# Moving one unit's cluster masks ahead of its products in four of a pair's six periods

## The chip, the cores and the metric

The kernel runs on one core of one Trainium2 chip. The metric is the device time of one execution in microseconds (us). Before the change the median of 3 runs is 947.51 us, from 947.37 to 947.69.

Five engines work beside each other on a core. PE is the matrix engine; the profile lists its weight loads apart, as PEld. DVE, ACT and POOL work on vectors, and SP issues most of the transfers. Each engine takes its instructions in the order in which they were written, and semaphores tie the engines together. PE multiplies a stationary operand (the weights, `lhsT`) with a moving one (`rhs`); the result goes to PSUM, where it can be added to what stands there (`start=False`). A matmul that contracts over 64 or 32 partitions takes 64 or 32 of the array's 128 rows only, so that two or four such matmuls in different rows can run at once. The profile writes the form of the weights as rows\*columns: 64\*128, 32\*128, 128\*32.

## The reference

Two blocks follow each other. The first is a clustered attention over 4 batches of 8 heads, with 768 positions of 64 values; the second is a gated feed-forward layer over the 3072 tokens, 512 to 2048 to 512, all in float32.

```python
q_assign = np.argmax(np.einsum('bhsd,hcd->bhsc', q_n, c_n), axis=-1)   # 16 clusters
k_assign = np.argmax(np.einsum('bhsd,hcd->bhsc', k_n, c_n), axis=-1)
mask = q_assign[:, :, :, None] == k_assign[:, :, None, :]
scores = scale * np.matmul(q, k.transpose(0, 1, 3, 2))
scores = np.where(mask, scores, -1000000000.0)
scores = scores - np.max(scores, axis=-1, keepdims=True)
attn = np.exp(scores)
attn = attn / (np.sum(attn, axis=-1, keepdims=True) + 1e-09)
out = np.matmul(attn, v)
...
h = x @ w_in
sp = np.maximum(h, 0.0) + np.log1p(np.exp(-np.abs(h)))
return (h * erf(sp)) @ w_out
```

## The kernel before

The attention works on 16 pairs of heads, numbered p from 0 to 15; the two heads of a pair lie in partitions 0 to 63 and 64 to 127 (`e` is 0 or 1). A pair has 12 units: a unit is one block of 128 keys (`j`) against one half of the queries (384 columns). A period handles two units, `u` and `u + 1`, so a pair has six periods, `i` from 0 to 5.

Per unit and head there are four steps on PE.

- `products` (line 546): the products of queries and keys, float32, 64 rows for each head, 384 columns. It opens the sum in the PSUM tile `sc` (`start=True`). A float32 matmul shows as two in the profile.
- `scores` (line 559): the cluster masks. `km` and `qm` hold, in bfloat16, one row for the shift (the negated maximum of the query's row) and rows that take a huge number off where the clusters differ. It adds to `sc` and closes it. With `rows=Q` it takes 32 rows for each head: rows 0 to 31 and 64 to 95. In the first period of all and in the last four it takes 64 (`rows=D`).
- `curve` (line 573): the exponential on ACT, from `sc` into `pr`.
- `attend` (line 594): the products with the values, weights of 128 rows and 32 columns, one period later. For every half, `divide` adds the products that give the sums and divides.

The shift needs the row maxima of the masked scores before the exact products exist. They are found ahead, by `maxima_step` (line 459), from a bfloat16 copy of queries and keys. A step has a pass of products (`qv` with `kv`, 64 rows for each head), then a mask pass (`qm` with `km`) onto the same PSUM tile `wide`, then a reduction on DVE that reads `wide`. Of `wide` there is one, so each step's first pass waits for the reduction of the step before. A period makes two steps. As first step of a period stands, in most periods, the remaining 256 keys of one block of queries, as second step the first 512 (or 384) of the next one. The steps run about seven ahead, so those of the later periods belong to the next pair, whose `qv`, `kv`, `qm` and `km` are other tiles.

`maxima_step` is a generator. With `behind=False` its mask pass takes 64 rows for each head. With `behind=True` it stops after the first pass, and its mask pass then takes rows 32 to 63 and 96 to 127 alone, where the masks lie a second time; so `scores` in rows 0 to 31 and 64 to 95 can run beside it.

The order of the work is written out by hand in `period` (line 1393); nothing plans it anew. On PE a period of the pairs 1 to 15 runs like this: the first step (both passes, 64 rows), `products(u)`, `products(u + 1)`, the second step's first pass, `scores(u)` beside the second step's mask pass, `scores(u + 1)`, and then `attend` of the two units before. Small masks of the next pair stand between (`masks`, line 429; table `MASKS`, line 55): in period 2 one between the two products in 64 rows, and one after `scores(u + 1)` in 32 rows (`turned<-hotT,pick`). The tile `sc` has two buffers, one for each unit of a period. Every call passes through a helper at line 127, so the profile shows that line for nearly everything; the names of the tiles tell the steps apart.

After the attention the feed-forward layer runs on PE with weights of 128 rows; the change does not touch it.

Of the kernel before, what the change touches and what calls it, by code (L numbers as in the profile page):

```python
# [9 lines left out]
F32 = mybir.dt.float32  # L10
# [9 lines left out]
P = 128  # L20
B, H, S, D = 4, 8, 768, 64
C = 16
NJ = S // P
Q = 32
NB = S // Q
HW = S // 2
QW = HW // 2
TW = QW + 1
HJ = NJ // 2
# [106 lines left out]
def kernel(  # L136
# [37 lines left out]
    def passing(name, bufs, **kw):  # L174
        return attention.enter_context(tc.tile_pool(name=name, bufs=bufs, **kw))

    ps_s = passing("ps_s", 2, space=PSUM)
# [30 lines left out]
    rows = [{nm: const.tile([P, S], F32, name=f"{nm}T{i}") for nm in "qk"} for i in range(2)]  # L208
# [124 lines left out]
    for e in range(2):  # L333
        for n in range(2):
            r = e * D + n * Q
# [37 lines left out]
    def transposes(p, which="qk"):  # L373

        if p >= NPAIR:
            return
        st = pairs[p]
        for nm in which:
            st[nm + "T"] = rows[p % 3][nm]
            ve.transpose(out=st[nm + "T"], in_=st.pop(nm).rearrange("p n t -> p (n t)"))  # L380
        if "k" in which:
            st.update(lows[p % 2])
            if p > 1:
                load_qk(p + 1)
# [44 lines left out]
    def masks(p, nm, half, bank, narrow=False, copied_by=ae):  # L429

        if p >= NPAIR:
            return lambda: None
        st = pairs[p]
        cols = slice(half * HW, (half + 1) * HW)
        r, hot = slice(0, D) if nm == "q" else slice(D, P), st["hotT"]
        picked = pick[r, half]
        if narrow:
            r = slice(r.start + Q, r.stop)
            picked = pick[r, 1]
            hot = hot if half else st["aside"]  # L440
        won = bank[:, 0:HW]
        te.matmul(won, lhsT=picked, rhs=hot[r], start=True, stop=True)
        if nm == "q":
            return lambda: ae.activation(out=st["qm"][:, cols], in_=won, func=ACT.Relu)
        if copied_by is ve:
            return lambda: ve.tensor_scalar(
                out=st["km"][:, cols], in0=won, scalar1=BIG, scalar2=nbig, op0=ALU.mult, op1=ALU.add
            )
        return lambda: ae.activation(
            out=st["km"][:, cols], in_=won, func=ACT.Identity, bias=nbig, scale=BIG  # L450
        )
# [3 lines left out]
    def pieces_of(i, keys_of):  # L455
        t, part = divmod(i, 2)
        return ((t, part, *((0, keys_of[t]), (keys_of[t], S))[part]),)
# [84 lines left out]
    units = [(p, half, j) for p in range(NPAIR) for half in range(2) for j in range(NJ)]  # L542

    sc_of = {}

    def products(u):
        p, half, j = units[u]
        if u in sc_of:
            return
        st = pairs[p]  # L550
        sc = sc_of[u] = ps_s.tile([P, 2, 512], F32, name="sc", tag="s")
        for e in range(2):
            r = slice(e * D, (e + 1) * D)
            te.matmul(
                sc[:, e, 0:HW], lhsT=st["kT"][r, j * P : (j + 1) * P],
                rhs=st["qT"][r, half * HW : (half + 1) * HW], start=True, stop=False,
            )

    def scores(u, rows=Q):

        p, half, j = units[u]
        st = pairs[p]
        sc = sc_of[u]
        assert ("shift", half) in st
        for e in range(2):
            r = slice(e * D, (e + 1) * D)
            r = slice(r.start, r.start + rows)
            te.matmul(
                sc[:, e, 0:HW], lhsT=st["km"][r, j * P : (j + 1) * P],
                rhs=st["qm"][r, half * HW : (half + 1) * HW], start=False, stop=True,  # L570
            )

    def curve(u):
# [795 lines left out]
    def run(work):  # L1369
        for _ in work:  # L1370
            pass
# [3 lines left out]
    def step_ahead(p, i, behind=False):  # L1375
        if p == 0 and i < NJ:
            steps = maxima_step(0, pieces_of(NJ + i, FIRST_KEYS), behind=behind, by_products=True)
        elif p == 0 and i < NJ + len(JOINED):
            steps = maxima_step(1, JOINED[i - NJ], behind=behind)
        else:  # L1380
            p, i = divmod(2 * NJ * p + NJ + 1 + i, 2 * NJ)
            steps = maxima_step(p, pieces_of(i, KEYS), behind=behind) if p < NPAIR else iter(())
        if not behind:
            run(steps)
        return steps
# [7 lines left out]
    def period(p, i):  # L1393
        u = 2 * NJ * p + 2 * i
        n1, n2 = 2 * p - 1, 2 * p
        early = lambda n: 0 <= n < N_EARLY

        def mask(place):
            which = (MASKS if p else FIRST_MASKS).get((i, place))
            if which:  # L1400
                return masks(p + 1, *which, turned[0 if i in (0, 5) else 1], place == 2)
            return lambda: None

        if u > 0:
            for which in turns if i in (0, 3) else ():
                turn(*which)
                turns.remove(which)
            if i == 3 and not p:
                transposes(2, "k")
            if i == 3 and p:  # L1410
                similarities(p + 2)
                routing[0] = choose(p + 2, turned[0], True)
            step_ahead(p, 2 * i)
            if i == 3 and p:
                next(routing[0], None)
            if i == 2:
                transposes(p + 2, "k" if p else "q")
        mask(0)()
        if i == 0 and early(n1 - 1):
            sign(n1 - 1)  # L1420
        elif i == 3 and early(n1):
            sign(n1)
        if i == 4:
            next(routing[0], None)
        next(part[0], None)
        if i == 0 and p:
            run(routing[0])
            transposes(p + 2, "q")
        if u == 2:
            next(routing[0])  # L1430
        products(u)
        mask(3)()
        products(u + 1)
        mask(1)()
        second = step_ahead(p, 2 * i + 1, True) if u > 0 else iter(())
        next(second, None)
        rows = D if u == 0 or u + NJ + 2 >= len(units) else Q
        scores(u, rows)
        next(second, None)
        next(second, None)  # L1440
        next(part[0], None)
        if i == 5 or u == 2:
            next(routing[0], None)
        scores(u + 1, rows)
        later = mask(2)
        if i == 3 and not p:
            similarities(p + 2)
            routing[0] = choose(p + 2, turned[0], True)
        if i == 0:
            later()  # L1450
            curve(u)
        else:
            curve(u)
            later()
        curve(u + 1)
        if u == 0:
            step_ahead(0, 1)
            similarities(1)
            routing[0] = choose(1, turned[1])
            next(routing[0])  # L1460
            vectors(1, "q")
            vectors(1, "k")
        if i == 0 and early(n1 - 1):
            bounded(n1 - 1)
            shifted(n1 - 1)
        elif i == 1 and early(n1):
            size_and_rest(n1)
        elif i == 5 and early(n2):
            rest(n2)
        for _ in range(FORMS.get(p, {}).get(i, 0)):  # L1470
            x_forms.pop(0)() if x_forms else forms.pop(0)[0]()
        if i == 3:
            if not p:
                next(routing[0], None)
            if early(n1):
                bounded(n1)
                shifted(n1)
        elif i == 1:
            load(p + 1, "v", v, vp)
            if p == 0:  # L1480
                run(routing[0])
        elif i == 4:
            vectors(p + 2, "k")
            vectors(p + 2, "q")
        if u > 0:
            if i == 1 and early(n1 - 1):
                summed(n1 - 1)
            elif i == 4 and early(n1):
                summed(n1)
            if i in POOL_FORMS.get(p, ()) and forms:  # L1490
                forms.pop(0)[1]()
            for w in (u - 2, u - 1):
                accumulate(w)
            for w in (u - 2, u - 1):
                attend(w)
            if i == 3:
                next(routing[0], None)
            if i % HJ == 0 and u - 1 != LATE or u - 3 == LATE:
                part[0] = divide(u - 1 - u % NJ)
                next(part[0])  # L1500
        if i == 3 and early(n2):
            size(n2)
# [11 lines left out]
    st = pairs[0]  # L1514
# [56 lines left out]
    u = len(units)  # L1571
# [13 lines left out]
    behind = pool("behind", 1).tile([P, 1], F32, name="behind")  # L1585
# [87 lines left out]
```

## Time and profile before

| what | value |
|---|---|
| median of the runs | 947.51 us |
| the profiled execution's own time | 948.0 us |
| its span, from first to last instruction | 946.3 us |
| granted PE clock | 1.00 |
| PE busy | 939.0 us (99% of the span) |
| DVE busy | 785.0 us (83%) |
| ACT busy | 547.2 us (58%) |
| POOL busy | 505.6 us (53%) |
| attention, first unit's products to the last period's | 8.9 to 396.0 us |
| six periods of one pair (p = 7 to p = 8) | 23.9 us |

A row of the timeline gives the start and the length in us, the engine, the operation, output and inputs by name, the weights' rows\*columns, the moving operand and how many such instructions were joined. The ends of matmuls are modelled and overlap with the next ones; so the text works with the differences of starts. Products with keys and queries that lie in the third set of buffers show as `sc<-more_out`.

### The profile page before, as it was taken

What the parts mean: (1) busy time and instruction counts of PE and PEld (TensorE: products, weight loads), DVE (VectorE), ACT (ScalarE), POOL (GpSimd) and SP (SyncE); (2) the same over time, 40 slices, a digit from 0 to 9 for tenths busy, and PEclk for the clock granted to TensorE, in tenths of its full rate; (3) what the DMA queues carried; (4) which work ended last, traced back from release to release, by engine and by line L of the source; (5) the groups of instructions that cost most, each with busy time, mean ns of one, the idle gap of its engine ahead of it and who ended that gap; (6) DMA issues with size and microseconds to landing.
All of it is one profiled execution on the core that took longest, in us unless ns stands there. A gap on an engine that the chain in (4) does not pass through costs nothing.

```text
span 946.3 us, 22340 instructions
## 1 busy us (share of the span) xinstructions
PE 939.0 (99%) x8764; PEld 708.1 (75%) x8764; DVE 785.0 (83%) x1420; ACT 547.2 (58%) x809; POOL 505.6 (53%) x357
## 2 busy tenths in 40 slices
PE   8999999999999999999999999999999999999998
PEld 3555555555555555588888888998999899989987
DVE  7888888888888887869886688689868977897887
ACT  3677777777777777476423543653257236525541
POOL 1688888888888888999118211450063016103600
PEclk9999999999999999999999999999999999999999
DMA  9354455445443621133876248353454336343533
GB/s 217 73 114 112 112 113 111 112 112 111 113 113 69 157 58 36 26 120 124 216 224 238 100 122 214 109 179 112 156 167 135 133 119 206 113 154 123 157 112 111
DMA packets 176352, 123.17 MB, mean 130 GB/s; under 512 B 132600, under 2 KB 143352, under 8 KB 176248
## 3 DMA queue, kind: packets, MB, share of 16 engines
q1 hardware_dynamic: 171880, 116.34, 43.1%
q0 software_dynamic: 1872, 4.98, 3.0%
q8 instruction: 69, 1.13, 0.5%
q10 hardware_dynamic: 2496, 0.43, 0.2%
q14 instruction: 35, 0.29, 0.1%
HBM read 91.78 MB, written 23.33 MB: 122 GB/s over the span
## 4 chain that ended last, share of the span: by engine, by line
PE 98%; DVE 1%; ACT 0%; issue 0%; DVEq 0%
PE bank L127 43%; PE turned L127 32%; PE sc L127 17%; PE wide L127 6%; DVE nmx L127 1%; ACT qm L127 0%; DVE sims L127 0%; ACT km L127 0%; DVE hotT L127 0%; DVE wide L127 0%; DVE hot L127 0%; DVE nbig L127 0%; DVE osb L127 0%; DVEq L1668 0%; DVE lowest L127 0%
## 5 line engine op out<-in xcount | busy, mean ns | idle before, releaser
L127 POOL TENSOR_TENSOR more_out<-more_out,pr 128x768 f32<-128x768 f32 x128 | 217.2, 1697 | 15.8 <-ACT pr L127 6.1
L127 DVE TENSOR_REDUCE nmx<-wide 128x2 f32<-128x512 f32 (+2 forms) x189 | 179.1, 948 | 46.9 <-PE wide L127 45.9
L127 ACT ACTIVATE pr<-sc 128x768 f32<-128x768 f32 x192 | 148.5, 810 | 80.5 <-PE wide L127 73.0
L127 PE MATMUL turned<-pr,in_v 128*32 128x193 f32 x3072 | 145.2, 330 | 0.0
L127 POOL TENSOR_TENSOR g<-g 128x512 f32<-128x512 f32 x36 | 47.2, 1310 | 180.7 <-DVE g L127 178.8
L127 PEld LDWEIGHTS turned<-pr,in_v 128*32 128x32 f32 x3072 | 90.2, 109 | 51.3 <-issue 27.3
L127 DVE TENSOR_TENSOR g<-g 128x512 f32<-128x512 f32 x132 | 90.8, 688 | 22.9 <-PE bank L127 12.2
L127 PE MATMUL sc<-qT,kT 64*128 64x384 f32 x528 | 98.5, 485 | 0.0
L127 DVE TENSOR_TENSOR g<-bank,g 128x256 f32<-128x256 f32 (+1 forms) x128 | 64.7, 531 | 18.1 <-PE bank L127 9.4
L127 PE MATMUL bank<-g_more,g 128*128 128x256 f32 (+1 forms) x328 | 75.8, 374 | 0.0
L127 PE MATMUL bank<-x_own,w_in 128*128 128x128 f32 (+1 forms) x440 | 74.0, 309 | 0.0
L127 ACT ACTIVATE a_s<-g 128x1024 f32<-128x1024 f32 x38 | 39.7, 1056 | 58.0 <-POOL g L127 45.3
L127 POOL TENSOR_TENSOR more_out<-pr,pr 128x768 f32<-128x768 f32 x32 | 59.6, 1864 | 20.1 <-ACT pr L127 20.1
L127 PEld LDWEIGHTS bank<-g_more,g 128*128 128x128 f32 x328 | 61.1, 190 | 8.4 <-DVE g L127 0.4
L127 DVE TENSOR_TENSOR g<-a_s,g 128x512 f32<-128x512 f32 x76 | 65.9, 888 | 0.9 <-ACT a_s L127 0.9
L127 PEld LDWEIGHTS bank<-x_own,w_in 128*128 128x128 f32 x440 | 63.2, 191 | 4.4 <-issue 0.6
L127 PE MATMUL wide<-kv,qv 64*128 64x256 bf16 (+2 forms) x378 | 64.8, 327 | 0.9 <-ACT km L127 0.6
L127 PE MATMUL bank<-w_out,g 128*128 128x256 f32 x280 | 64.5, 379 | 0.0
L127 PEld LDWEIGHTS <-qv 64*128 64x128 bf16 x384 | 23.1, 93 | 52.8 <-issue 37.8
L127 PE MATMUL wide<-km,qm 64*128 64x256 bf16 (+4 forms) x378 | 62.3, 326 | 0.0
L127 ACT ACT_TABLE_LOAD x40 | 51.3, 1283 | 17.6 <-DVE g L127 17.0
L127 PEld LDWEIGHTS sc<-qT,kT 64*128 64x128 f32 x528 | 46.3, 187 | 19.1 <-issue 1.8
(244 smaller groups left out, 1993.0 us busy)
## 6 DMA issues: line engine op xcount, KB each, us to landing
g_more<-b_dram SPq DMA_DIRECT2D x52, 512.0 KB
g_more<-w_dram SPq DMA_DIRECT2D x84, 256.0 KB
x_own<-in_moe_w_in_dram SPq DMA_DIRECT2D x13, 512.0 KB
in_v<-in_v_dram SPq DMA_DIRECT2D x32, 192.0 KB
x_dram<-more_out SPq DMA_DIRECT2D x128, 48.0 KB
x_own<-x_dram SPq DMA_DIRECT2D x6, 1024.0 KB
in_k<-in_k_dram SPq DMA_DIRECT2D x59, 96.0 KB
in_q<-in_q_dram SPq DMA_DIRECT2D x58, 96.0 KB
```

What stands on the lines that cost most here:

```text
L127: ins = getattr(self.engine, name)(*args, **kw)
```

## The change

`scores` may now open the sum in `sc` (`ahead=True`: `start=True`, `stop=False`), and `products` may close it (`behind=True`). In `period` a flag `ahead` is true for p > 0 in the periods 1, 2, 4 and 5, as long as the units left are more than eight. There the first maxima step is made with `behind=True` as well: after its first pass come the masks of unit `u` (`scores(u, Q, True)`) in rows 0 to 31 and 64 to 95, and beside them the step's mask pass in rows 32 to 63 and 96 to 127 instead of in 64 rows. `products(u, True)` then adds to `sc` and closes it. In the block after the products, the second step's mask pass now has `scores(u + 1)` beside it, and no second pair of masks follows. The numbers of instructions stay as they are on every engine; only PE's order changes. The periods 0 and 3, pair 0 and the last four periods are as before.

```diff
+    def score_banks(u):
+        if u not in sc_of:
+            sc_of[u] = ps_s.tile([P, 2, 512], F32, name="sc", tag="s")
+        return sc_of[u]
+
-    def products(u):
+    def products(u, behind=False):
         p, half, j = units[u]
-        if u in sc_of:
+        if u in sc_of and not behind:
             return
         st = pairs[p]
-        sc = sc_of[u] = ps_s.tile([P, 2, 512], F32, name="sc", tag="s")
+        sc = score_banks(u)
...
-                rhs=st["qT"][r, half * HW : (half + 1) * HW], start=True, stop=False,
+                rhs=st["qT"][r, half * HW : (half + 1) * HW], start=not behind, stop=behind,
...
-    def scores(u, rows=Q):
+    def scores(u, rows=Q, ahead=False):
...
-                rhs=st["qm"][r, half * HW : (half + 1) * HW], start=False, stop=True,
+                rhs=st["qm"][r, half * HW : (half + 1) * HW], start=ahead, stop=not ahead,
...
+        more = u + NJ + 2 < len(units)
+        ahead = p > 0 and i % HJ > 0 and more
...
-            step_ahead(p, 2 * i)
+            step = step_ahead(p, 2 * i, ahead)
+            next(step, None)
+            if ahead:
+                scores(u, Q, True)
+            run(step)
...
-        products(u)
+        products(u, ahead)
         mask(3)()
         products(u + 1)
         mask(1)()
         second = step_ahead(p, 2 * i + 1, True) if u > 0 else iter(())
         next(second, None)
-        rows = D if u == 0 or u + NJ + 2 >= len(units) else Q
-        scores(u, rows)
+        rows = Q if u > 0 and more else D
+        scores(u + ahead, rows)
         next(second, None)
         next(second, None)
...
-        scores(u + 1, rows)
+        if not ahead:
+            scores(u + 1, rows)
```

More of the change, by code (lines that the diff above doesn't have):

```diff
@@ L555, in products @@
                 sc[:, e, 0:HW], lhsT=st["kT"][r, j * P : (j + 1) * P],
-                rhs=st["qT"][r, half * HW : (half + 1) * HW], start=True, stop=False,
+                rhs=st["qT"][r, half * HW : (half + 1) * HW], start=not behind, stop=behind,
             )
-    def scores(u, rows=Q):
+    def scores(u, rows=Q, ahead=False):
         p, half, j = units[u]
         st = pairs[p]
-        sc = sc_of[u]
+        sc = score_banks(u)
         assert ("shift", half) in st
```

## The prediction

> **What bounds the kernel now.** I read the page first: who is busy, at what clock, and what the chain that ended last consists of.
>
> ```profile
> span 946.3 us, 22340 instructions
> PE 939.0 (99%) x8764; PEld 708.1 (75%) x8764; DVE 785.0 (83%) x1420; ACT 547.2 (58%) x809; POOL 505.6 (53%) x357
> PE 98%; DVE 1%; ACT 0%; issue 0%; DVEq 0%
> ```
>
> PE carries 98% of that chain. Then the busy time by stretches inside the attention, and the waits between 45 and 385 us:
>
> ```profile
> 200.00:250.00 50.00, 50.00 (x703) 26.38 (x703) 43.11 (x73) 38.24 (x58) 43.79 (x28) 1.00 0.51 112
> ...
> PEld L127 <- issue: 66.4, 180, 0.6
> DVE nmx L127 <- PE wide L127: 42.7, 63, 1.5
> PEld turned L127 <- issue: 24.4, 72, 0.4
> ```
>
> The first row gives the stretch, its length, and the busy time of PE, PEld, DVE, ACT and POOL, then the granted clock. PE is busy for 50.00 of 50 us at a clock of 1.00, while DVE (43.11), ACT (38.24) and POOL (43.79) have room. DVE waits for PE (`nmx <- wide`), and matmuls wait for no engine for long; only weight loads stand still, by "issue", for 66.4 and 24.4 us. So in this stage a period is as long as PE's sequence. A busy PE isn't PE at its peak, so the starts inside one period have to say what that sequence is made of. This is PE in period 5 of pair 7, up to the next period's first pass; then its weight loads:
>
> ```profile
> 207.53 0.28 PE L127 MATMUL wide<-kv,qv 64*128 64x256 bf16 x2
> 207.65 0.27 PE L127 MATMUL wide<-km,qm 64*128 64x256 bf16 x2
> 207.75 1.46 PE L127 MATMUL sc<-qT,kT 64*128 64x384 f32 x8
> 209.05 0.38 PE L127 MATMUL wide<-kv,qv 64*128 64x512 bf16 x2
> 209.36 0.34 PE L127 MATMUL sc<-qm,km 32*128 32x384 bf16 x2
> 209.37 0.39 PE L127 MATMUL wide<-km,qm 32*128 32x512 bf16 x2
> 209.53 0.33 PE L127 MATMUL sc<-qm,km 32*128 32x384 bf16 x2
> 209.79 1.51 PE L127 MATMUL turned<-pr,in_v 128*32 128x193 f32 x32
> 211.23 0.28 PE L127 MATMUL wide<-kv,qv 64*128 64x256 bf16 x2
> ```
>
> ```profile
> 207.52 0.10 PEld L127 LDWEIGHTS <-qv 64*128 64x128 bf16 x2 [0.31 <-issue]
> ...
> 207.65 0.95 PEld L127 LDWEIGHTS sc<-qT,kT 64*128 64x128 f32 x8
> 208.73 0.26 PEld L127 LDWEIGHTS <-qv 64*128 64x128 bf16 x2
> 209.35 0.09 PEld L127 LDWEIGHTS <-km 32*128 32x128 bf16 x2 [0.36 <-issue]
> 209.78 0.32 PEld L127 LDWEIGHTS turned<-pr,in_v 128*32 128x32 f32 x12 [0.32 <-issue]
> ```
>
> Two things are to be seen. First, what a stream costs when the form of the weights stays: 256 columns take 0.10 to 0.12 us (207.53 to 207.65 to 207.75), 384 columns 0.17 (209.36 to 209.53), so 512 about 0.21 (by proportion). Second, what it costs when the form changes. The 512-column pass from 209.05 should end at 209.26, and the next matmul, in form 32\*128, starts at 209.36: 0.10 more. The 384 columns from 209.53 should end at 209.70, and `attend` in form 128\*32 starts at 209.79: 0.09. Every weight load of a new form has an "issue" wait before it (0.31, 0.36, 0.32 us) and starts with its matmul; loads of the same form, such as `qT,kT` at 207.65, were made under the matmul before. So a **change of form** empties the array, and three kinds of it (128\*32 to 64\*128, 64\*128 to 32\*128, 32\*128 to 128\*32) cost some 0.09 to 0.10 us each.
>
> The same numbers stand in the first and the last of the 57 periods that change (14 pairs by four, and period 1 of pair 15):
>
> ```profile
> 47.92 0.28 PE L127 MATMUL wide<-kv,qv 64*128 64x256 bf16 x2
> 48.15 1.46 PE L127 MATMUL sc<-qT,kT 64*128 64x384 f32 x8
> 49.44 0.38 PE L127 MATMUL wide<-kv,qv 64*128 64x512 bf16 x2
> ...
> 382.08 0.28 PE L127 MATMUL wide<-kv,qv 64*128 64x256 bf16 x2
> 382.31 1.46 PE L127 MATMUL sc<-qT,kT 64*128 64x384 f32 x8
> 383.61 0.38 PE L127 MATMUL wide<-kv,qv 64*128 64x512 bf16 x2
> ```
>
> 0.23 us for the first step and 1.29 to 1.30 for the products in both.
>
> **The change part by part.** No instruction is added or removed on any engine; the transfers and SP's and POOL's queues keep their order. All of the cost lies on PE.
>
> *The first step's two passes, with the masks in them.* Now 0.22 to 0.23 us. After: the first pass (0.12), a change 64\*128 to 32\*128 (0.095), a block in 32 rows that lasts as long as its longest member, 384 columns of `scores(u)` (0.17; the 256 columns of the step's own masks lie beside them), and a change 32\*128 to 64\*128 for the products. No row shows that fourth kind. Its nearest rows are the other three, 0.09 to 0.10; I take 0.095, and keep nothing as the low end. Sum 0.48, so **+0.25 us**.
>
> *The products.* They now come first after a change of form. That price stands in the last pair, whose last periods make no maxima step:
>
> ```profile
> 387.73 1.51 PE L127 MATMUL turned<-pr,in_v 128*32 128x193 f32 x32
> 389.18 1.56 PE L127 MATMUL sc<-qT,kT 64*128 64x384 f32 x8
> 390.57 0.49 PE L127 MATMUL sc<-qm,km 64*128 64x384 bf16 x4
> ...
> 389.17 0.95 PEld L127 LDWEIGHTS sc<-qT,kT 64*128 64x128 f32 x8 [0.31 <-issue]
> ```
>
> The same eight matmuls take 1.39 us there (389.18 to 390.57) against 1.29 to 1.30: float32 weights load longer, and after a change nothing hides the first load. **+0.10 us**, low end nothing, should the load slip under the 32-row block.
>
> *The second block.* Now 0.43 us from 209.36 to 209.79: 384 columns, 384 again in the same rows, a change. After: 512 columns of the step's masks with `scores(u + 1)` beside, 0.01 until they start, 0.01 for the load and a change: 0.33. **-0.10 us**. But in period 2 the little mask of the next pair follows in the rows of the step's mask pass:
>
> ```profile
> 220.97 0.34 PE L127 MATMUL sc<-qm,km 32*128 32x384 bf16 x2
> 220.97 0.33 PE L127 MATMUL wide<-km,qm 32*128 32x384 bf16 x2
> 221.14 0.32 PE L127 MATMUL sc<-qm,km 32*128 32x384 bf16 x2
> 221.15 0.32 PE L127 MATMUL turned<-hotT,pick 32*128 32x384 bf16 x1
> 221.40 1.51 PE L127 MATMUL turned<-pr,in_v 128*32 128x193 f32 x32
> ```
>
> It lies beside the second masks (221.14 and 221.15) and ends last. It still does with those gone, so the 14 periods 2 save nothing.
>
> *What waits.* `scores(u)` needs its `sc` buffer some 0.02 us sooner than the products do now. The exponentials that free it are long done, and unit `u`'s will start earlier, as its sum is closed by the products. The `wide` tile gets tighter: the reduction starts when the second mask pass is done, and `attend`, which covers it, now starts 0.10 us sooner.
>
> ```profile
> 209.80 1.23 DVE L127 TENSOR_REDUCE nmx<-wide 128x2 f32<-128x1024 f32 x1 [0.42 <-PE wide L127]
> ...
> 384.49 1.21 DVE L127 TENSOR_REDUCE nmx<-wide 128x2 f32<-128x1024 f32 x1
> ...
> 384.35 1.51 PE L127 MATMUL turned<-pr,in_v 128*32 128x193 f32 x32
> 385.79 0.28 PE L127 MATMUL wide<-kv,qv 64*128 64x256 bf16 x2
> ```
>
> It ends at 211.03, and the next pass starts at 211.23: 0.20 us of room becomes 0.10. At 384.49 it ends 0.09 before the pass at 385.79, which still starts 1.44 us after `attend`, as at 209.79 to 211.23. So I cost this at nothing; if 0.10 were too little, the saving of the second block would be lost. Between the two reductions DVE gains time, since the masks of the one and of the other move apart.
>
> *The sum.* 57 x (0.25 + 0.10) - 43 x 0.10 = 19.95 - 4.3 = 15.7 us; with 0.26 for the first part, which the 0.22 of 207.53 to 207.75 gives, 16.2. I take 16.0. The profiled execution took 948.0 us, 1.7 more than its span; that gives 964.0. The median, 947.51, lies 0.5 below it: **963.5 us**. Nothing later gives it back, as the feed-forward part starts when the attention has ended.
>
> The Trainium skill speaks of the unseen fourth kind (TensorEngine Tiling (Array Packing), Key Properties): changing the tiling mode, and not just the tile, drains the engine. By that rule both new changes drain, and the sum stays at 963.5; the three kinds in the rows agree with it, at 0.09 to 0.10 us.
>
> **The rivals.**
>
> *The products' load hides* under the block in 32 rows. For it: same-form loads are always hidden. Against it: all loads of a new form in the rows start with their matmul. It takes 57 x 0.10 = 5.7 off: 957.8.
>
> *The way back is free*: 32 to 64 rows needs no emptying, and the load hides as well. 57 x (0.095 + 0.10) = 11.1 off: 952.4.
>
> *Not slower: neither new change empties the array.* The weights of the 32-row block would go in while the 64-row pass streams, since this form only splits the same rows. Then a further 57 x 0.095 = 5.4 goes: 947.0, no change that can be measured. It decides as soon as both changes cost less than 0.03 us. Even so the gain is small: 0.06 us are lost in the first step for 0.10 won in the second block, and in period 2 nothing is won. Against it stands the wait of 0.36 us at 209.35, for this very change.
>
> The Trainium skill has a rule for this rival (TensorE: Matmul & The Clock Gate, Part 3, The mechanism): a load whose rows don't conflict, or that goes to the background buffer, is pulled ahead of running matmuls. By that rule the 0.36 us before the `km` load at 209.35 should not be there; the trace disagrees where the form changes.
>
> *A new wait*: the tightened `wide` takes back what the second block saves. 43 x 0.10 = 4.3 on top: 967.8. Against it stands the 0.09 that sufficed at 385.79.
>
> **How the numbers follow.** Forecast (961.5 to 966) 0.70, hidden load 0.09, free way back 0.06, new wait 0.08, no emptying at all 0.04; 0.03 are left for a gain that I can't name, as the units' exponentials come earlier. About 0.2% (1.9 us) is what a measurement of this kernel tells from no change. Faster 0.03, same 0.04, slower 0.93. The range from 957.3 to 968 takes in the hidden load and the new wait, and leaves 0.13 out.
>
> **What the profile after would show.** In the changed periods the first pass should be followed by `sc<-qm,km` in form 32\*128 some 0.21 us later, the products 0.27 after that, and the products should last 1.39. The block after them to `attend` should take 0.33 (0.43 in period 2). A period such as the one quoted grows from 3.70 to about 3.95, and period 2 by 0.35. "Issue" waits of PEld gain 57 or more before `km` and before `qT,kT`. ACT's first exponential starts some 0.8 us sooner in its period where ACT is free, and nothing comes of it. I would be wrong if the products after the 32-row block still took 1.30, or started with the block's end; or if a reduction of DVE held the next pass.

## The result, and the profile after

The changed kernel takes 962.69 us (median, 962.57 to 962.87), the one before 947.6 (947.37 to 947.69): a ratio of 1.016 with an interval of 1.0142 to 1.0177. It is slower by 15.1 us; the forecast was 963.5.

Three lines of the page of the changed kernel:

```profile
span 960.9 us, 22309 instructions
PE 953.4 (99%) x8764; PEld 713.5 (74%) x8764; DVE 782.1 (81%) x1420; ACT 552.3 (57%) x809; POOL 504.8 (53%) x357
...
PE 98%; DVE 1%; DMA 0%; SPq 0%; ACT 0%; issue 0%; DVEq 0%
```

The span has grown by 14.6 us, PE's busy time by 14.4, and that of no other engine by more than 6. (In the profile before, the attention's first products start 0.41 us later, at 8.93 us against 8.52; from there to the start of the last `attend` instruction the growth is 15.1.) PE stays the bound, at the same granted clock of 1.00. PE's timeline of period 4 of pair 7, and the first pass of the next:

```profile
210.38 0.28 PE L127 MATMUL wide<-kv,qv 64*128 64x256 bf16 x2
210.59 0.34 PE L127 MATMUL sc<-qm,km 32*128 32x384 bf16 x2
210.60 0.28 PE L127 MATMUL wide<-km,qm 32*128 32x256 bf16 x2
210.86 1.56 PE L127 MATMUL sc<-qT,kT 64*128 64x384 f32 x8
212.25 0.38 PE L127 MATMUL wide<-kv,qv 64*128 64x512 bf16 x2
212.57 0.34 PE L127 MATMUL sc<-qm,km 32*128 32x384 bf16 x2
212.57 0.39 PE L127 MATMUL wide<-km,qm 32*128 32x512 bf16 x2
212.89 1.51 PE L127 MATMUL turned<-pr,in_v 128*32 128x193 f32 x32
214.34 0.28 PE L127 MATMUL wide<-kv,qv 64*128 64x256 bf16 x2
```

From the first pass to the masks in 32 rows there are 0.21 us, from there to the products 0.27, the products take 1.39, and the second block 0.32. The first part has grown from 0.23 to 0.48, the products from 1.29 to 1.39, and the block has shrunk from 0.43 to 0.32. A period of 3.71 us takes 3.96. The waits of PE's weight loads between 45 and 413 us (engine, line, what was waited for; us in total, times, longest) hold the new ones:

```profile
PEld L127 <- issue: 73.6, 189, 0.6
PEld turned L127 <- issue: 23.0, 76, 0.4
PEld sc L127 <- issue: 10.1, 59, 0.3
PEld turned L127 <- DVE turned L127: 3.2, 14, 0.2
...
```

`PEld sc <- issue` is new in this size: 59 times, of which 57 are the float32 loads after the 32-row blocks; in the kernel before it stands there twice. Before `km`, where the prediction told of 57 more such waits, the list hardly grows: `PEld <- issue` has 189 instead of 184. The `km` load at 210.59 has no wait in the view, since it comes only 0.12 us after the load before it (210.37 and 0.10), and a wait that short isn't listed. So the price of this change is read from the starts, not from this list. The 14 waits for `turned` on DVE lie before `attend` in period 4 and cost nothing: the way to `attend` takes 0.324 us in the periods 1 and 5 as well.

The differences of starts, put together over the pairs 1 to 14 (medians of the 14 starts in the trace, ns precision, us):

| period | first part | products | second pass to block | block to `attend` | `attend` to next period | whole |
|---|---|---|---|---|---|---|
| 1, 4, 5 before | 0.229 | 1.292 | 0.312 | 0.427 | 1.447 | 3.707 |
| 1, 4, 5 after | 0.480 | 1.394 | 0.315 | 0.324 | 1.447 | 3.960 |
| 2 before | 0.228 | 1.298 | 0.412 | 0.433 | 2.124 | 4.496 |
| 2 after | 0.480 | 1.401 | 0.411 | 0.434 | 2.092 | 4.817 |
| 3 before | 0.336 | 1.290 | 0.312 | 0.484 | 1.797 | 4.219 |
| 3 after | 0.335 | 1.290 | 0.312 | 0.484 | 1.772 | 4.193 |

43 x 0.253 + 14 x 0.321 - 14 x 0.026 = 15.0 us, of the 15.1 measured. So the whole difference lies in these periods.

### The profile page after: what moved, and what is told of

Its sections match the earlier page's. It is cut to its first block, busy times and chain, and to the rows that moved or that the text cites. A ratio compares the mean times of both kernels' runs of the same rounds, so it can differ in the third digit from the quotient of the medians.

```text
span 960.9 us, 22309 instructions
## 1 busy us (share of the span) xinstructions
PE 953.4 (99%) x8764; PEld 713.5 (74%) x8764; DVE 782.1 (81%) x1420; ACT 552.3 (57%) x809; POOL 504.8 (53%) x357
## 4 chain that ended last, share of the span: by engine, by line
PE 98%; DVE 1%; DMA 0%; SPq 0%; ACT 0%; issue 0%; DVEq 0%
PE bank L127 42%; PE turned L127 32%; PE sc L127 19%; PE wide L127 5%; DVE nmx L127 0%; DMA in_k<-in_k_dram 0%; SPq L127 0%; DVE kT L127 0%; ACT qm L127 0%; DVE sims L127 0%; ACT km L127 0%; DVE hotT L127 0%; DVE wide L127 0%; DVE hot L127 0%; DVE osb L127 0%
## 5 line engine op out<-in xcount | busy, mean ns | idle before, releaser
L127 ACT ACTIVATE pr<-sc 128x768 f32<-128x768 f32 x192 | 153.1, 811 | 68.6 <-PE wide L127 35.9
L127 PE MATMUL sc<-qT,kT 64*128 64x384 f32 x528 | 102.4, 499 | 0.0
L127 PE MATMUL wide<-km,qm 32*128 32x256 bf16 (+5 forms) x378 | 62.7, 329 | 0.0
```

The lines of the kernel that those rows point to most:

```text
L127: ins = getattr(self.engine, name)(*args, **kw)
```

## The experiments

The theory: the loss consists of two changes of the weights' form (64 to 32 rows and back) and of a float32 load that comes first after a change; the overlap itself works and saves a little. The rivals: masks that open the sum, or products that close it, cost by themselves; or the blocks in 32 rows are what is slow. The medians of the first four runs stand against 947.55 us for the kernel before, measured beside them.

**The change of form alone.** In the kernel before, in the same 57 periods:

```diff
-            step_ahead(p, 2 * i)
+            run(step_ahead(p, 2 * i, p > 0 and i % HJ > 0 and u + NJ + 2 < len(units)))
```

> Edit: the kernel before, but in the same 57 periods the first maxima step's mask pass takes rows 32 to 63 and 96 to 127 instead of 64 rows for each head; no unit's masks are moved, and nothing lies beside that pass. Theory (changes of the weights' form): first pass 0.12, change 0.095, 256 columns 0.11 to 0.12, change 0.09: the products start 0.42 to 0.43 us after the first pass instead of 0.23, and take 1.39 instead of 1.29; the second block stays at 0.43. 57 x 0.30 = 17 us: 963.5 to 965, more than the whole change costs. Rival (the cost lies in the moved masks: the sum in PSUM is opened by them, or the 384 columns are simply longer than the 256): nothing was moved, so 947 to 948.

Measured: 964.51 us, a ratio of 1.018 (1.0163 to 1.0196). PE's timeline of this kernel, one changed period:

```profile
211.00 0.28 PE L127 MATMUL wide<-kv,qv 64*128 64x256 bf16 x2
211.21 0.28 PE L127 MATMUL wide<-km,qm 32*128 32x256 bf16 x2
211.42 1.56 PE L127 MATMUL sc<-qT,kT 64*128 64x384 f32 x8
212.81 0.38 PE L127 MATMUL wide<-kv,qv 64*128 64x512 bf16 x2
213.13 0.34 PE L127 MATMUL sc<-qm,km 32*128 32x384 bf16 x2
...
213.56 1.19 PE L127 MATMUL turned<-pr,in_v 128*32 128x193 f32 x24
```

First part 0.42, products 1.39, second block 0.43 as before: with nothing moved and the same columns, the loss is 17.0 us. The rival that lays it on the moved masks has fallen. The moved masks even give something back: the changed kernel is 1.8 us faster than this one, 43 x (0.103 - 0.054) from the two blocks, less some tenths in the periods 2.

**The masks ahead without a change of form.** In the changed kernel:

```diff
-            step = step_ahead(p, 2 * i, ahead)
-            next(step, None)
+            step_ahead(p, 2 * i)
             if ahead:
-                scores(u, Q, True)
-            run(step)
+                scores(u, D, True)
```

> Edit: the changed kernel, but the masks that go ahead take 64 rows for each head, after the first step's mask pass, which takes 64 rows as before; so the first part of the period has no change of form. Theory: first part 0.23 + 0.16 (384 columns) = 0.39 us, products 1.29, second block 0.325 (0.43 in period 2). 43 x 0.06 + 14 x 0.16 = 4.8 us, less up to 0.8 that comes back in the waits of periods 2 and 3: 951.5 to 952.5. Rival (masks that open the sum, and products that close it, cost by themselves): as much as the changed kernel or more, 962 to 966.

Measured: 951.69 us, a ratio of 1.0044 (1.0029 to 1.0059). PE's timeline of this kernel, one changed period up to its second step:

```profile
209.29 0.28 PE L127 MATMUL wide<-kv,qv 64*128 64x256 bf16 x2
209.41 0.27 PE L127 MATMUL wide<-km,qm 64*128 64x256 bf16 x2
209.52 0.33 PE L127 MATMUL sc<-qm,km 64*128 64x384 bf16 x2
209.68 1.45 PE L127 MATMUL sc<-qT,kT 64*128 64x384 f32 x8
210.97 0.38 PE L127 MATMUL wide<-kv,qv 64*128 64x512 bf16 x2
```

The masks open the sum here too, and the products close it, in 1.29 us (209.68 to 210.97). So the order of adding costs nothing. What remains is 0.16 us for the 384 columns ahead, against 0.10 saved behind.

**The step's masks first.** In the changed kernel, the first step's mask pass beside the unit's masks now opens `wide` at the start of the period, and the step's bfloat16 products follow:

```diff
+        if masks_first:
+            passes("qm", "km", True, slice(Q, D))
+            passes("qv", "kv", False, slice(0, D))
...
-            step = step_ahead(p, 2 * i, ahead)
-            next(step, None)
             if ahead:
                 scores(u, Q, True)
-            run(step)
+            run(step_ahead(p, 2 * i, ahead, ahead))
```

> Edit: the changed kernel with the first step's two passes in the other order: at the start of the period the unit's masks and beside them the step's masks, in 32 rows, and then the step's bfloat16 products in 64 rows, before the float32 products. The block beside each other stays, but attend now goes over to 32 rows instead of 64, so that one change of form is added and not two, and the first load after it is a bfloat16 one. Theory: first part 0.17 + 0.095 + 0.12 = 0.385 us against 0.48 in the changed kernel, products 1.29 against 1.39, second block as in the changed kernel. 43 x 0.055 + 14 x 0.155 = 4.5 us over the kernel before: 951.5 to 952.5. Rival (masks beside each other in 32 rows are what is slow, or the earlier masks): 961 to 963.

Measured: 951.50 us, a ratio of 1.0042 (1.0027 to 1.0057). PE's timeline of this kernel, one changed period up to its second step:

```profile
209.28 0.34 PE L127 MATMUL sc<-qm,km 32*128 32x384 bf16 x2
209.28 0.28 PE L127 MATMUL wide<-km,qm 32*128 32x256 bf16 x2
209.54 0.28 PE L127 MATMUL wide<-kv,qv 64*128 64x256 bf16 x2
209.66 1.46 PE L127 MATMUL sc<-qT,kT 64*128 64x384 f32 x8
210.96 0.38 PE L127 MATMUL wide<-kv,qv 64*128 64x512 bf16 x2
```

The same masks in the same 32 rows, beside each other as the changed kernel has them; but the first part takes 0.39 instead of 0.48 and the products 1.29 instead of 1.39 (medians; the rows shown give 0.38 and 1.30). Since `attend` goes over into the 32-row block, one change of form is saved, and a bfloat16 pass comes first after the other. That is worth 11.2 us. So the blocks in 32 rows aren't slow in themselves. Against the kernel before, this order is still 4.0 us slower.

**The same order, nothing moved.** The kernel before, with the mask pass of the first step in 32 rows and ahead of its products (`masks_first` in `maxima_step` as above), in the 57 periods:

```diff
-            step_ahead(p, 2 * i)
+            ahead = p > 0 and i % HJ > 0 and u + NJ + 2 < len(units)
+            run(step_ahead(p, 2 * i, ahead, ahead))
```

> Edit: as the run that takes 32 rows alone, but with the step's two passes in the other order: its masks in 32 rows right after attend, then its bfloat16 products in 64 rows, then the float32 products; no unit's masks are moved. One change of form more than before instead of two, and no float32 load behind it. Theory: first part 0.11 + 0.095 + 0.12 = 0.33 us against 0.23, all else as before: 57 x 0.10 = 5.7 us: 952.5 to 953.5. Against the run that takes 32 rows alone it measures one change and one bare float32 load: 0.195 us in 57 periods, 11 us. Rival: 947 to 948, as nothing is moved.

Measured: 953.23 us, a ratio of 1.0060 (1.0045 to 1.0075). In PE's timeline of this kernel the first part is 0.33 us (210.08 to 210.41), and the products take 1.29:

```profile
210.08 0.28 PE L127 MATMUL wide<-km,qm 32*128 32x256 bf16 x2
210.29 0.28 PE L127 MATMUL wide<-kv,qv 64*128 64x256 bf16 x2
210.41 1.46 PE L127 MATMUL sc<-qT,kT 64*128 64x384 f32 x8
211.70 0.38 PE L127 MATMUL wide<-kv,qv 64*128 64x512 bf16 x2
```

One further change of form alone costs 5.7 us in 57 periods, 0.10 each. Against the run that takes 32 rows alone it is 11.28 us, 0.198 in each period, for one change and one bare float32 load.

**The load by itself.** In the last two periods of pair 15 in the kernel before:

```diff
+        if at_end:
+            scores(u, D, True)
+            scores(u + 1, D, True)
-        products(u)
+        products(u, at_end)
         mask(3)()
-        products(u + 1)
+        products(u + 1, at_end)
...
-        scores(u, rows)
+        if not at_end:
+            scores(u, rows)
...
-        scores(u + 1, rows)
+        if not at_end:
+            scores(u + 1, rows)
```

> Edit: the kernel before, but in the last two periods of pair 15, where attend is followed at once by the float32 products, the masks of both units go ahead of the products, in 64 rows as they are there; nothing else is moved. The number of changes of form stays, and only the load that comes first after the change is another: bfloat16 instead of float32. Theory: the products of these two periods take 1.29 us instead of 1.39, the four masks before them 0.33 to 0.34 as before, so that a period of 3.26 us from products to products falls to 3.16; on the whole time 0.2 us, too little to be told from no change. Rival (the 0.10 us belong to the change of form, whatever is loaded after it): the products 1.29, but the masks ahead of them 0.43, and the period stays at 3.26.

Measured: 947.65 us in one run, against 947.9 in one run of the kernel before, both on another chip. The times alone tell nothing; PE's timeline does. The kernel with this edit, and below it the kernel before (the same profile as above; the granted clock was 1.00 in both):

```profile
392.43 0.50 PE L127 MATMUL sc<-qm,km 64*128 64x384 bf16 x4
392.77 1.45 PE L127 MATMUL sc<-qT,kT 64*128 64x384 f32 x8
394.15 1.51 PE L127 MATMUL turned<-pr,in_v 128*32 128x193 f32 x32
```

```profile
392.44 1.56 PE L127 MATMUL sc<-qT,kT 64*128 64x384 f32 x8
393.83 0.49 PE L127 MATMUL sc<-qm,km 64*128 64x384 bf16 x4
394.25 1.51 PE L127 MATMUL turned<-pr,in_v 128*32 128x193 f32 x32
```

From the first matmul after the change of form to `attend` there are 1.72 us instead of 1.81. With the edit the masks take 0.34 (392.43 to 392.77) and the products, with the next change behind them, 1.38. Before, the products took 1.39 without a change behind them, and the masks with it 0.42. So the two changes cost what they did, and the 0.10 us of the first load are gone: they belong to the float32 load, not to the change. The next period, the last, shows the same.

## Why the prediction was right

*PE's sequence is the period.* Right: the sum of the differences of starts gives 15.0 of the 15.1 us.

*The first part, +0.25 us.* Right: 0.229 became 0.480. The kind of change that no row had shown, 32\*128 to 64\*128, costs what its neighbours cost: the 384 columns from 210.59 should end at 210.76, and the products start at 210.86. The rule of the Trainium skill on changes of the tiling mode (TensorEngine Tiling (Array Packing), Key Properties) held for it, and the rival of a free way back has fallen. For one of the three kinds that it takes as known, 128\*32 to 64\*128, the prediction shows a wait (0.31 us) but no price; in the changed kernel's trace the last group of the division starts at 210.12, such a group takes 0.16, and the next pass starts at 210.38, so it is 0.10 too.

*The products, +0.10.* Right: 1.292 became 1.394. The rival in which the load slips under the 32-row block has fallen. Two rows of the weight loads in the changed kernel's timeline show why; the first is the load of the products, which began with its matmul at 210.86, after 0.17 us in which no load ran:

```profile
210.86 0.95 PEld L127 LDWEIGHTS sc<-qT,kT 64*128 64x128 f32 x8 [0.17 <-issue]
212.56 0.09 PEld L127 LDWEIGHTS <-km 32*128 32x128 bf16 x2 [0.53 <-issue]
```

The second row is the load for the block after the products: it came 0.53 us after the last load, with its matmul at 212.57, although it needs half the rows. The rule of the Trainium skill that loads are pulled ahead where rows don't conflict, or where they go to the background buffer (TensorE: Matmul & The Clock Gate, Part 3, The mechanism), brought no load of a new form ahead here: in the attention of every run the first of them starts at most 0.03 us before its matmul. The rival "neither change empties the array" has fallen with it.

*The second block, -0.10 in 43 periods and nothing in 14.* Right: 0.427 became 0.324, and in period 2 0.433 became 0.434.

*What waits.* The tightened `wide` held no pass: `attend` to the next pass took 1.447 us before and after. The rival of a new wait has fallen.

*Nothing comes of the earlier exponentials.* This step was wrong, by 0.4 us, and with it "matmuls wait for no engine for long": two short waits stood in the kernel before, in its weight loads between 45 and 396 us.

```profile
PEld turned L127 <- DVE den L127: 4.4, 14, 0.3
...
PEld turned L127 <- ACT km L127: 2.6, 13, 0.2
```

Neither stands in the list of the changed kernel. In period 2, products for the next pair (`turned<-qT,ccT`) waited for ACT to copy a mask out of that bank; with the first exponential earlier ACT is there in time, and 0.03 us a pair come back. In the two runs without masks ahead this stayed (2.12 us from `attend` to the next period), in the three with masks ahead it went (2.09). In period 3 the wait for `den` on DVE shrank by 0.025 us a pair, in all five kernels whose periods 1 and 2 are longer, masks ahead or not; so I put it down to the longer periods, which no run tests by itself. Together 14 x 0.057 = 0.8 us, the distance between the forecast and the measurement. These 0.8 us were left out of the sum; its other terms stand, and together they measure 15.9 us against the 16.0 taken.

*Not slower.* This rival fell because both changes cost their price. How small the gain would be without them is an estimate, as no run takes them away: 43 x (0.10 - 0.06) - 14 x 0.06, about 1 us, and at most the 0.8 us of waits. The run with the masks ahead in 64 rows doesn't measure this: it adds no change of form, but lays nothing beside the masks that go ahead, and came out 4.1 us slower than the kernel before.

## What to carry to other kernels

Two matmuls beside each other in separate rows save the shorter one's columns, but going over to that form and back empties the array twice; here that cost 0.095 us each time and 0.10 for the float32 load that then came first, to hide 256 columns of 0.11 us. Count the changes of form in a sequence first, put blocks of one form where the form changes anyway, and let a bfloat16 pass, not a float32 one, come first after a change; here that took back 11.2 of the 15.1 us. Where the form changes, look at whether the weight load starts with its matmul. The list of "issue" waits shows the longer of these places only: in the run that takes 32 rows alone, `PEld sc <- issue` stands twice, as before the change, though each of the 57 float32 loads there waits 0.12 us.

## What the runs showed of the hardware

The 0.10 us stood in the forecast; that they hang on the load, and not on the change, took the last run to show. A float32 load that comes first after a change of form delays its first pair of matmuls by 0.10 us, a bfloat16 load by 0.01 (first pass to the next pass 0.12 us where it streams for 0.11). And a sum in PSUM that small masks open and float32 products close runs as fast as the other way round: 1.290 us for the products against 1.292.
